# Order of the first key units, halves of a key weight block, a layer norm and a query unit moved, and a bank of its own for the last output columns

## The chip, the cores and the metric

The kernel runs on one core of a Trainium2 chip. The metric is the device time of one execution in microseconds (us). One core has no second die to compare with, so every run here is of one state ("fast" in the records); what remains is a spread of 1 to 2 us between executions of the same kernel. Each number of a kernel is a median of 5 or 6 runs (11 for the kernel before in all calls but the first) unless the text says otherwise. A ratio is the record's own estimate from the fast runs of one call, with its 95% interval; it is not quite the ratio of the medians or of the means quoted.

Names: PE is TensorE's matmul side, PEld its weight load, DVE VectorE, ACT ScalarE, SP the engine that issues most DMAs. In the program a "key unit (i, c)" is eight matmuls that multiply tile i of x (128 rows, normalised and transposed) by block c (512 columns) of the key weights. Value ("V") units are the same with blocks 2 and 3. An "eviction" takes a result out of PSUM, the memory that PE writes, which the program uses in banks of 512 columns; the eviction of a key unit is called "phi" (two instructions on ACT, `e_sb` and `r_sb`, the latter a relu, then two on DVE). psA, psB and psX are tiles in PSUM. The "V run" is the group of products that starts with the first psA near 31 us; xs are sums and differences of blocks of x that DVE makes for it, and a "weight sum" (`w_sums`) is the same for weights.

## The reference, cut to what matters

```python
h  = x + A(layernorm(x))          # linear attention: qkv projection, phi, kv sums, output projection
h2 = h + B(layernorm(h))          # token MLP: w1, gelu, w2
# x: (1, 2048, 1024); wqkv: (1024, 3072); w1: (2048, 3584); w2: (3584, 2048); all bf16
```

The change touches the first 25 us (layer norm of the first four tiles and their key units), two points between 25 and 45 us, and the last product of the second MLP matrix. The rest of the program's instruction order is the same in both kernels.

## The kernel before: the parts that matter

The head. Tiles 0 to 3 are normalised on DVE, transposed on PE, copied out of PSUM, and multiplied. "pin" fixes the program order on every engine.

```python
xs = {0: load_x(0, True)}; xs[1] = load_x(1)
for k0 in (0, hk):                                   # key block 0, in halves of 512 KB
    nc.sync.dma_start(wkv[:, k0:k0 + hk, 0:CW], wqkv_v[:, k0:k0 + hk, D:D + CW])
for i in range(2, 4):
    xs[i] = load_x(i)
for c in range(1, 2 * NDC):                          # key block 1 whole (1 MB), then the V blocks
    nc.sync.dma_start(wkv[:, :, c * CW:(c + 1) * CW], wqkv_v[:, :, D + c * CW:D + (c + 1) * CW])
# ... (tiles 4 and 5 after c == 1; then the query weights)

warm_up(10)
# ... statistics and normalisation of tile 0
transpose_in(0)                  # 8 PE transposes; first copy on ACT, second on DVE
pin(ln[1][1](1)); pin(ln[1][2]()); stats(1)
k_parts(0, 0, lo_k)              # first four matmuls of unit (0,0)
# ... normalise tile 1
transpose_in(1)
phis = [k_parts(0, 0, hi_k)]     # last four
for i in (1, 2):
    # ... statistics of tile i + 1
    phis.append(k_parts(i, 0))
    # ... normalise tile i + 1
    transpose_in(i + 1)
    # ... (i == 2: evictions, and the first weight sum on DVE)
    phis.append(k_parts(i - 1, 1))
# ... proj_unit(3, 0), w_sums, ln_stats(4), proj_unit(2, 1), load_biases
ln_finish(G0)                    # ACT: Ln, Exp of tile 4; DVE: normalise; DMA transpose
proj_unit(3, 1, pin)
# ... two PSUM buffers from here on
proj_unit(0, NDC, pin)           # V unit
```

Later, ahead of the V run:

```python
ln_finish(G0 + 2)
load_next(2 * G0)
q_fill()                         # a query unit and its two ACT evictions
```

The last product, cut into 384 and 128 columns in one PSUM bank:

```python
def m7(self, cuts=(0, CW)):
    for a, b in zip(cuts, cuts[1:]):
        self.mm(7, self.X, False, True, cols=slice(a, b))
        self.evac(0, 0, self.X, a, b)
# ...
pend.m7((0, CW - P, CW))
```

## Time and profile before

| | before |
|---|---|
| time, first three runs | 581.31 us (580.81 to 581.78) |
| span of the profiled execution | 578.7 us |
| PE busy | 569.4 us, 98% |
| PE not busy | 9.3 us |

The head of the page of the kernel before (busy us, share of the span, instructions, by engine):

```profile
span 578.7 us, 7486 instructions
PE 569.4 (98%) x2832; PEld 267.2 (46%) x2854; DVE 385.7 (67%) x752; ACT 211.9 (37%) x432; POOL 1.8 (0%) x8
```

PE is the limit, and a change that removes no matmul can only close its gaps. The list of waits of PE in the kernel before names them (total us, times, longest):

```profile
PE tp L668 <- DVE xn L402: 2.0, 2, 1.0
...
PE psX L228 <- DVE ot_5119 L193: 0.7, 1, 0.7
PE psB L499 <- ACT psB L512: 0.5, 1, 0.5
PE acc_t L423 <- ACT r_sb L161: 0.4, 1, 0.4
```

PE's timeline of the kernel before (start, duration, operation, count, and in brackets the idle time ahead of it with what ended it) places them:

```profile
6.05 0.72 PE L668 MATMUL tp<-ident,xn 128*128 128x128 bf16 x8 [0.98 <-DVE xn L402]
7.13 1.04 PE L423 MATMUL acc_t<-wkv,xnT 128*128 128x512 bf16 x4 [0.35 <-ACT xnT L678]
9.15 0.72 PE L668 MATMUL tp<-ident,xn 128*128 128x128 bf16 x8 [0.98 <-DVE xn L402]
9.71 2.75 PE L423 MATMUL acc_t<-wkv,xnT 128*128 128x512 bf16 x12
...
26.08 5.34 PE L423 MATMUL acc_t<-wkv,xnT 128*128 128x512 bf16 x24 [0.36 <-ACT r_sb L161]
31.26 1.03 PE L499 MATMUL psA<-wkv,xnT 128*128 128x512 bf16 x4
...
45.08 1.02 PE L499 MATMUL psB<-pqT,xs 128*128 128x512 f16 x4 [0.55 <-ACT psB L512]
...
571.61 2.44 PE L228 MATMUL psX<-gO,sa 128*128 128x384 f16 x14
574.76 0.94 PE L228 MATMUL psX<-gO,sa 128*128 128x128 f16 x14 [0.71 <-DVE ot_5119 L193]
```

A 512-column matmul is drawn 0.379 us long, but in a stream the next one starts 0.216 us later: 12 matmuls from 9.71 are drawn as 2.75, that is 11 x 0.216 + 0.379. The Trainium skill gives both lengths ("TensorE: Matmul & The Clock Gate", sections "Single matmul latency" and "Back-to-back issue gap": (398 + 512)/2.4 = 379 ns, and 512/2.4 + 2.5 = 216 ns), and this trace agrees with both. Only the 216 ns is a measurement, though: by its own legend the profile models the ends of matmuls, so the 0.379 us is how long it draws them.

### The profile page before, as it was taken

The page shows a single profiled execution, that of the slowest core. Times are in us where ns is not written, and L with a number is a line of the kernel's source. Part 1 is how long each engine was busy: PE and PEld are TensorE (multiplying, and loading weights), DVE is VectorE, ACT ScalarE, POOL GpSimd, SP SyncE. Part 2 cuts the span into 40 slices and gives each one's busy share as a digit, 9 for nine tenths or more (in the row PEclk, how much of TensorE's full clock was granted, in tenths as well). Part 3 has the DMA queues.
Part 4 walks back from the last instruction along what each step waited for, and adds up shares of the span by engine and source line. Part 5 has one row for each costly group of instructions (what it writes and reads, how often), then busy time and mean ns, then how long its engine had stood idle before and what let it go on. Part 6 is the DMA issues. An engine that isn't in the chain of part 4 may idle for free.

```text
span 578.7 us, 7486 instructions
## 1 busy us (share of the span) xinstructions
PE 569.4 (98%) x2832; PEld 267.2 (46%) x2854; DVE 385.7 (67%) x752; ACT 211.9 (37%) x432; POOL 1.8 (0%) x8
## 2 busy tenths in 40 slices
PE   7999999999999999999999999999999999999997
PEld 3444444455555444444444444444444444444443
DVE  6897887556767889876666666567765456455543
ACT  4647777656668777333222322223000000000000
POOL 1000000000000000000000000000000000000000
PEclk9999999999999999999999999999999999999999
DMA  8943431139438952242224322204966436521101
GB/s 283 361 83 75 91 73 37 20 116 271 69 73 172 283 165 92 73 129 72 74 80 126 85 74 72 74 0 109 226 193 172 130 100 172 149 78 46 36 28 36
DMA packets 109811, 66.55 MB, mean 115 GB/s; under 512 B 31810, under 2 KB 101712, under 8 KB 109776
## 3 DMA queue, kind: packets, MB, share of 16 engines
q1 hardware_dynamic: 109568, 65.94, 42.8%
q8 instruction: 22, 0.36, 0.3%
q10 hardware_dynamic: 144, 0.13, 0.1%
q14 instruction: 13, 0.11, 0.1%
q0 software_dynamic: 64, 0.01, 0.0%
HBM read 50.34 MB, written 8.39 MB: 101 GB/s over the span
## 4 chain that ended last, share of the span: by engine, by line
PE 96%; DVE 2%; ACT 1%; issue 0%; DMA 0%
PE psX L228 17%; PE psW L228 17%; PE psZ L228 17%; PE acc_t L904 9%; PE acc_t L757 9%; PE psY L228 8%; PE psB L499 4%; PE psA L499 4%; PE psC L499 4%; PE acc_t L423 3%; PE psE L499 2%; PE nd_ps L855 1%; DVE st L392 1%; PE kvps_464 L452 1%; PE kvps_465 L452 0%
## 5 line engine op out<-in xcount | busy, mean ns | idle before, releaser
L228 PEld LDWEIGHTS <-sa 128*128 128x128 f16 x1134 | 110.5, 98 | 132.5 <-issue 0.9
L223 DVE TENSOR_TENSOR sa<-w1p 128x1024 f16<-128x1024 bf16 x70 | 47.9, 685 | 20.0 <-PE psX L228 12.4
L757 PE MATMUL acc_t<-xnT,wq_sb 128*128 128x512 bf16 x248 | 57.1, 379 | 0.3
L904 PE MATMUL acc_t<-wo_sb,pqT 128*128 128x512 bf16 x250 | 55.7, 379 | 0.3
L223 DVE TENSOR_TENSOR sa<-w2p 128x1792 f16<-128x1792 bf16 x40 | 43.4, 1084 | 10.1 <-PE psW L228 7.6
L904 PEld LDWEIGHTS <-pqT 128*128 128x128 bf16 x256 | 24.8, 98 | 29.1
L757 PEld LDWEIGHTS <-wq_sb 128*128 128x128 bf16 x256 | 24.5, 98 | 27.4
L164 DVE TENSOR_SCALAR e_sb<-e_sb 128x512 bf16<-128x512 bf16 x64 | 18.5, 290 | 26.9 <-ACT e_sb L160 26.4
L264 DVE TENSOR_TENSOR tt<-psW,dd 128x512 f32<-128x512 f32 x22 | 15.2, 692 | 29.2 <-PE psW L228 29.2
L228 PEld LDWEIGHTS <-w1p 128*128 128x128 bf16 x224 | 21.9, 98 | 26.4
L228 PEld LDWEIGHTS <-w2p 128*128 128x128 bf16 x224 | 21.9, 98 | 26.4
L259 DVE TENSOR_TENSOR psY<-psX,dd 128x512 f32<-128x512 f32 x22 | 15.4, 699 | 27.5 <-PE psX L228 27.5
L160 ACT ACTIVATE e_sb<-acc_t 128x512 bf16<-128x512 f32 x40 | 23.9, 597 | 24.2 <-PE acc_t L757 20.7
L499 PEld LDWEIGHTS <-xs 128*128 128x128 f16 x208 | 20.0, 98 | 23.6 <-DVE xs L485 0.8
L269 DVE TENSOR_TENSOR tt<-tt,psZ 128x512 f32<-128x512 f32 x22 | 15.1, 688 | 18.0 <-PE psZ L228 17.9
L228 PE MATMUL psZ<-hT_2226,w1p 128*128 128x512 f16 x112 | 26.8, 379 | 0.0
L499 PE MATMUL psA<-wkv,xnT 128*128 128x512 bf16 x98 | 26.4, 379 | 0.3
L228 PE MATMUL psW<-hE,sa 128*128 128x512 f16 x112 | 26.6, 379 | 0.0
L228 PE MATMUL psX<-hT_2225,sa 128*128 128x512 f16 x112 | 26.6, 379 | 0.0
L228 PE MATMUL psW<-hT_2227,w1p 128*128 128x512 f16 x112 | 26.5, 379 | 0.0
L228 PE MATMUL psZ<-hO,sa 128*128 128x512 f16 x112 | 26.5, 379 | 0.0
L228 PE MATMUL psX<-hO,sa 128*128 128x512 f16 x112 | 26.5, 379 | 0.0
(256 smaller groups left out, 838.9 us busy)
## 6 DMA issues: line engine op xcount, KB each, us to landing
w1p<-in_B_w_dram SPq DMA_DIRECT2D x14, 1024.0 KB, 5.6
w2p<-in_B_w_dram SPq DMA_DIRECT2D x8, 1792.0 KB, 8.1
xr<-in_A_x_dram SPq DMA_DIRECT2D x16, 256.0 KB, 3.4
x_sb<-in_A_x_dram SPq DMA_DIRECT2D x15, 256.0 KB, 4.1
wkv<-in_A_wqkv_dram SPq DMA_DIRECT2D x3, 1024.0 KB, 9.7
wq_sb<-in_A_wqkv_dram SPq DMA_DIRECT2D x2, 1024.0 KB, 12.6
wo_sb<-in_A_wo_dram SPq DMA_DIRECT2D x2, 1024.0 KB, 6.5
wkv<-in_A_wqkv_dram SPq DMA_DIRECT2D x2, 512.0 KB, 5.7
```

Of the source, the lines that this page charges most:

```text
L160: pin(nc.scalar.activation(e_sb[:], src, ACT.Exp))
L164: pin(nc.vector.tensor_scalar(e_sb[:], e_sb[:], 1.0, PHI_EPS, ALU.min, ALU.add))
L223: return nc.vector.tensor_tensor(t, a, b, op)
L228: nc.tensor.matmul(ps[:, cols], lhsT=sa[:, k, :], rhs=mv(k)[:, cols], start=(start and k == 0), stop=(stop and k == self.nk - 1), skip_gro ...
L259: nc.vector.tensor_tensor(self.Y[:], self.X[:], self.d[:], ALU.add)
L264: nc.vector.tensor_tensor(self.t[:], self.W[:], self.d[:], ALU.add)
L269: nc.vector.tensor_tensor(self.t[:], self.t[:], self.Z[:], ALU.subtract)
L392: return nc.vector.bn_stats(st[:, c, :], x_sb[:, c * CW:(c + 1) * CW])
L423: mm = nc.tensor.matmul(pp[:, 0:CW], lhsT=xnT[:, kt, i * P:(i + 1) * P], rhs=wkv[:, kt, c * CW:(c + 1) * CW], start=(kt == 0), stop=(kt == ...
L499: pin(nc.tensor.matmul(ps[:], lhsT=lhs[:, k, :], rhs=rhs[:, k, :], start=(start and k == 0), stop=(k == hk2 - 1), skip_group_check=True,))
L757: nc.tensor.matmul(qp[:, 0:SW], lhsT=wq_sb[:, kt, j * P:(j + 1) * P], rhs=xnT[:, kt, u * SW:(u + 1) * SW], start=(kt == 0), stop=(kt == ND ...
L904: nc.tensor.matmul(ap_[:, 0:CW], lhsT=pqT[:, j, i * P:(i + 1) * P], rhs=wo_sb[:, j, dc * CW:(dc + 1) * CW], start=(j == 0 and not SEED_RES ...
```

## The change

The intent: give PE work while it waits for the second tile's normalisation (all of unit (0,0), and an order in which key units lie between the groups of transposes); make unit (0,1) possible earlier by loading key block 1 in two halves ahead of tile 3; take two waits of PE for ACT away by moving a layer norm and a query unit; and let the last 128 columns run without waiting for the eviction of the 384 ahead of them.

```diff
-        def m7(self, cuts=(0, CW)):
-            for a, b in zip(cuts, cuts[1:]):
-                self.mm(7, self.X, False, True, cols=slice(a, b))
-                self.evac(0, 0, self.X, a, b)
+        def m7(self):
+            for a, b, ps in self.parts:      # parts: (0, 384, X), (384, 512, tile of its own)
+                self.mm(7, ps, False, True, cols=slice(a, b))
+                self.evac(0, 0, ps, a, b)
 ...  (m5 adds into each part; only the last product is cut)
+            xs[2] = load_x(2)
+            for k0 in (0, hk):
+                nc.sync.dma_start(wkv[:, k0:k0 + hk, CW:D], wqkv_v[:, k0:k0 + hk, D + CW:2 * D])
+            for i in range(3, G0 + 2):
+                xs[i] = load_x(i)
 ...  (V blocks and query weights follow)
-                    pin((nc.vector.tensor_copy if i == 0 and h == 1 else nc.scalar.copy)(*t))
+                    pin(nc.scalar.copy(*t))
 ...
-            k_parts(0, 0, lo_k)
+            k_unit(0, 0)
             ...  normalise tile 1
             transpose_in(1)
+            ln_stats(2); stats(2)
+            k_unit(1, 0)
+            norm_halves(2); phi_act((0, 0))
+            k_unit(0, 1)
+            phi_act((1, 0))
+            transpose_in(2)
+            ln_stats(3); stats(3)
+            phi_dve((0, 0)); w_sums(kmov, slice(0, 1)); norm_halves(3)
+            phi_dve((1, 0)); phi_act((0, 1))
+            k_unit(1, 1)
+            transpose_in(3)
 ...  (then units (2,0), (3,0), (2,1), (3,1))
             load_biases(trp)
-            ln_finish(G0)
             proj_unit(3, 1, pin)
 ...
             proj_unit(0, NDC, pin)
+            ln_finish(G0)
 ...
+            q_fill()
             ln_finish(G0 + 2)
             load_next(2 * G0)
-            q_fill()
```

More of the change, by code (lines that the diff above doesn't have):

```diff
@@ L265, in m4, with m5 @@
             self.evac(1, 0, self.W)
-        def m5(self):
+        def m5(self, cut=None):
             self.mm(5, self.Z, False, True)
             nc.vector.tensor_tensor(self.t[:], self.t[:], self.Z[:], ALU.subtract)
-            nc.vector.tensor_tensor(self.X[:], self.X[:], self.t[:], ALU.add)
+            self.parts = [(0, CW, self.X)]
+            if cut is not None:
+                self.parts = [(0, cut, self.X), (cut, CW, psw.tile([P, BANK], F32, tag="w", name="psX2"))]
+            for a, b, ps in self.parts:
+                nc.vector.tensor_tensor(ps[:, a:b], self.X[:, a:b], self.t[:, a:b], ALU.add)
             self.evac(0, 1, self.Z)
@@ L275, in m6 @@
             self.evac(1, 1, self.Y)
-        def m7(self, cuts=(0, CW)):
-            for a, b in zip(cuts, cuts[1:]):
-                self.mm(7, self.X, False, True, cols=slice(a, b))
-                self.evac(0, 0, self.X, a, b)
+        def m7(self):
+            for a, b, ps in self.parts:
+                self.mm(7, ps, False, True, cols=slice(a, b))
+                self.evac(0, 0, ps, a, b)
     def moving(E, O, T1, T3, T4):
@@ L292, in moving, with run_pair @@
         }
-    def run_pair(st, nxt, split, pending):
+    def run_pair(st, nxt, split, pending, cut=None):
         if split:
@@ L311, in run_pair @@
             nxt.asum(2)
-        st.m5()
+        st.m5(cut)
         if nxt is not None:
@@ L649 @@
             )
-            for i in range(2, 4):
+            xs[2] = load_x(2)
+            for k0 in (0, hk):
+                nc.sync.dma_start(wkv[:, k0:k0 + hk, CW:D], wqkv_v[:, k0:k0 + hk, D + CW:2 * D])
+            for i in range(3, G0 + 2):
                 xs[i] = load_x(i)
-            for c in range(1, 2 * NDC):
+            for c in range(2, 2 * NDC):
                 nc.sync.dma_start(wkv[:, :, c * CW:(c + 1) * CW], wqkv_v[:, :, D + c * CW:D + (c + 1) * CW])
-                if c == 1:
-                    for i in range(G0, G0 + 2):
-                        xs[i] = load_x(i)
             for c in range(NDC):
@@ L661 @@
             halves = (slice(0, CW), slice(CW, D))
-            ln[0] = ln_chunks(0, xs.pop(0))
             def transpose_half(i, h):
@@ L688, with norm_halves, phi_act, phi_dve @@
             pps = {}
-            pin(ln[0][1](0))
-            pin(ln[0][1](1))
-            pin(ln[0][2]())
+            def norm_halves(i):
+                for h in range(2):
+                    pin(ln[i][4](halves[h]))
+            def phi_act(*keys):
+                for key in keys:
+                    phis[key][0]()
+            def phi_dve(*keys):
+                for key in keys:
+                    phis[key][1]()
+            def k_unit(i, c):
+                phis[i, c] = k_parts(i, c)
+            phis = {}
+            ln_stats(0)
             stats(0)
@@ L694 @@
             pin(ln[1][1](0))
-            for h in range(2):
-                pin(ln[0][4](halves[h]))
+            norm_halves(0)
             transpose_in(0)
@@ L700 @@
             stats(1)
-            k_parts(0, 0, lo_k)
-            for h in range(2):
-                pin(ln[1][4](halves[h]))
+            k_unit(0, 0)
+            norm_halves(1)
             transpose_in(1)
-            phis = [k_parts(0, 0, hi_k)]
-            for i in (1, 2):
-                ln[i + 1] = ln_chunks(i + 1, xs.pop(i + 1))
-                pin(ln[i + 1][1](0))
-                pin(ln[i + 1][1](1))
-                pin(ln[i + 1][2]())
-                stats(i + 1)
-                phis.append(k_parts(i, 0))
-                for h in range(2):
-                    pin(ln[i + 1][4](halves[h]))
-                phis[2 * i - 2][0]()
-                if i == 2:
-                    phis[1][0]()
-                transpose_in(i + 1)
-                if i == 2:
-                    phis[0][1]()
-                    phis[1][1]()
-                    w_sums(kmov, slice(0, 1))
-                phis.append(k_parts(i - 1, 1))
-            phis[2][1]()
-            for act, dve in phis[3:]:
-                act()
-                dve()
-            proj_unit(3, 0, pin)
-            w_sums(kmov, slice(1, 2))
+            ln_stats(2)
+            stats(2)
+            k_unit(1, 0)
+            norm_halves(2)
+            phi_act((0, 0))
+            k_unit(0, 1)
+            phi_act((1, 0))
+            transpose_in(2)
+            ln_stats(3)
+            stats(3)
+            phi_dve((0, 0))
+            w_sums(kmov, slice(0, 1))
+            norm_halves(3)
+            phi_dve((1, 0))
+            phi_act((0, 1))
+            k_unit(1, 1)
+            transpose_in(3)
+            phi_dve((0, 1))
+            k_unit(2, 0)
+            phi_act((1, 1))
+            phi_dve((1, 1))
+            k_unit(3, 0)
+            phi_act((2, 0))
+            phi_dve((2, 0))
+            w_sums(kmov, slice(1, 2))
+            k_unit(2, 1)
+            phi_act((3, 0))
+            phi_dve((3, 0))
+            phi_act((2, 1))
+            phi_dve((2, 1))
             ln_stats(G0)
-            proj_unit(2, 1, pin)
             load_biases(trp)
-            ln_finish(G0)
             proj_unit(3, 1, pin)
@@ L1015 @@
         cur.evac.prefetch()
-        run_pair(cur, nxt, False, pend)
+        run_pair(cur, nxt, False, pend, None if nxt is not None else CW - P)
         pend = cur
         cur = nxt
-    pend.m7((0, CW - P, CW))
+    pend.m7()
 _INS = ['A_x', 'A_wqkv', 'A_wo', 'B_x', 'B_w1', 'B_b1', 'B_w2', 'B_b2']
```

## The prediction

> **What bounds it now.** TensorE. The page gives PE 569.4 us busy of a 578.7 us span (98%) at full granted clock; the chain that ended last is 96% PE. The change removes no matmul, so only PE's 9.3 us of gaps can shrink. The list of waits and PE's timeline show those in reach: 1.0 us before the second tile's transposes (at 9.15, waiting for its normalisation) and about 0.4 us hidden in the groups around it; 0.36 us at 26.08 (a V unit waits for ScalarE's relu); 0.55 us at 45.08 (psB waits for ScalarE's copy); 0.71 us in the last product (128 columns wait for the eviction of 384). Together 3.0 us, 0.5%.
>
> **What the change does, costed.**
> 1. Tail. The last 128 columns get their own bank; their 14 matmuls (0.94 us) no longer wait for the 0.62 us eviction: gain 0.6 to 0.7. The Trainium skill, "PSUM — Partial Sum Buffer", section "PSUM bank collisions raise a hardware error", says two engines may not touch one bank at once even at disjoint columns; the trace shows that wait, 0.71 us at 574.76.
> 2. Head. Unit (0,0) now lies wholly before the second transposes and fills the 1.0 us hole; tile 0's second copy moves from DVE to ACT, freeing DVE 0.8 us earlier. New gaps: (a) unit (0,0)'s second half needs the second half of the first weight block, landing about 8.4 (DMA view): about 0.4 us. (b) Unit (1,0) follows its own transposes at once and exposes a copy: 0.35 to 0.45. (c) Tile 3's load now queues behind 1 MB of weights. That block took 3.0 us (x 3 landed 9.7, the block 12.7), so x 3 lands about 12.7. Then, in DVE order, statistics 1.3, aggregate 0.2, a phi pair 0.7, a weight sum 1.2, half a normalisation 0.4: tile 3's transposes at about 16.6, while PE is free at about 15.8; 0.5 to 1.0 us lost. The skill, "DMA: Bandwidth & Descriptors", section "Queues, rings and completion order", says an engine takes a row's descriptors in order; the landings agree. Half loads let unit (0,1) start at 11.9 (half lands about 10.6). Net of the head: between 0.5 lost and 1.0 gained, most likely 0.
> 3. LayerNorm of tile 4 finishes one V unit later: removes the 0.36 us.
> 4. The query unit ahead of tile 6's LayerNorm lets ScalarE do two evictions inside its 2.9 us wait for statistics: psB's copy comes earlier, gains 0.45.
>
> **Total.** 0.65 + 0 + 0.36 + 0.45, about 1.4 us: **580.0 us**, range **578.8 to 581.0**. Faster by over 2% (11.6 us) would exceed all of PE's idle time: 0.01. Within 2%: 0.98. Slower by over 2%: 0.01.
>
> **What would show it.** PE's timeline: no wait inside the last product; no idle at the first V units and at psB near 44; unit (0,0) as eight matmuls with a short DMA wait in the middle; a copy wait before unit (1,0); idle before tile 3's transposes, put down to DVE's normalisation. DVE's timeline: tile 3's first statistics at about 12.7, released by DMA. PE busy the same within 1 us.
>
> **What would make it wrong.** x 3 landing before the block ahead of it (1 us more gained, 579); the second weight half arriving after unit (0,1) reaches it (1 us lost, 581); ScalarE's new order only moving its waits to the next PSUM reuse; the last output's DMA, not the matmuls, setting the end.

## The result, and the profile after

In the first call: 579.30 us (579.17 to 580.38, 6 runs) against 581.00 us (580.59 to 581.78, 6 runs); ratio 0.9973, 95% interval 0.9960 to 0.9986. The changed kernel was run in two more calls, with ratios 0.9985 (0.9974 to 0.9997) and 0.9985 (0.9968 to 1.0002). Over its 17 runs the median is 579.89 us. So the gain is real but small, somewhere between 0.8 and 1.7 us, 1.3 us if the means of all runs are taken (579.96 against 581.26, the latter over 39 runs of the kernel before). The prediction was 580.0. Part of the spread is PE's clock: the record lists the granted clock of each run but those of the kernel before in the first call, and runs at 0.994 to 0.997 are slower than the others of their kernel (the kernel before: 582.0 us over 10 such runs, 581.0 over 23 at 0.999 or 1.000). At 0.999 or 1.000 the changed kernel takes 579.60 us (13 runs), which is 1.4 us less. This figure does not show everything: it reads 1.000 for the profile of tail_mid (below), whose first four matmuls of unit (0,0) took 1.89 us, against 1.04 us in tail_mid_again.

The profile after fell in the slowest of its six runs (580.38 us), in which the first weights landed late. Compare it with the profile before by stretches, not by absolute times. Head of the page and PE's list of waits, kernel after:

```profile
span 578.6 us, 7489 instructions
...
PE acc_t L427 <- DMA wkv<-in_A_wqkv_dram: 1.6, 2, 1.2
...
PE tp L670 <- DVE xn L406: 0.9, 2, 0.5
PE acc_t L427 <- ACT xnT L680: 0.5, 1, 0.5
PE psB L503 <- DVE xs L489: 0.3, 1, 0.3
```

The waits for ACT's relu, for psB's copy and for the eviction of the last product are gone. In their place stand waits for weights, for a copy, and for xs. PE's timeline of the kernel after:

```profile
8.27 1.02 PE L427 MATMUL acc_t<-wkv,xnT 128*128 128x512 bf16 x4 [1.25 <-DMA wkv<-in_A_wqkv_dram]
9.67 1.02 PE L427 MATMUL acc_t<-wkv,xnT 128*128 128x512 bf16 x4 [0.37 <-DMA wkv<-in_A_wqkv_dram]
10.53 0.61 PE L670 MATMUL tp<-ident,xn 128*128 128x128 bf16 x8
11.59 3.41 PE L427 MATMUL acc_t<-wkv,xnT 128*128 128x512 bf16 x15 [0.45 <-ACT xnT L680]
...
17.75 0.72 PE L670 MATMUL tp<-ident,xn 128*128 128x128 bf16 x8 [0.35 <-DVE xn L406]
...
32.36 1.03 PE L503 MATMUL psA<-wkv,xnT 128*128 128x512 bf16 x4
...
36.34 1.04 PE L503 MATMUL psB<-wo_sb,xs 128*128 128x512 f16 x4 [0.28 <-DVE xs L489]
...
572.46 2.44 PE L228 MATMUL psX<-gO,sa 128*128 128x384 f16 x14
574.73 0.94 PE L228 MATMUL psX_5224<-gO,sa 128*128 128x128 f16 x14
```

The first line is bad luck of this run: in the profile before, the same half of block 0 had landed 1.5 us sooner (5.0 us after its issue instead of 6.5) and unit (0,0) began at 7.13. The next lines are the new order. The hole of 1.0 us before the second transposes is filled. But unit (0,0) now waits in its middle for the second half of block 0; unit (1,0) waits for the copy of its own transposes; and tile 3's transposes wait for DVE. DVE's timeline of the kernel after shows why tile 3's transposes wait:

```profile
14.02 1.29 DVE L396 BATCH_NORM_STATS2 st<-x_sb 128x6 f32<-128x512 bf16 x2 [0.79 <-DMA x_sb<-in_A_x_dram]
...
16.15 1.22 DVE L477 TENSOR_TENSOR pqT<-wkv 128x2048 f16<-128x2048 bf16 x1
17.28 0.73 DVE L406 TENSOR_SCALAR xn<-x_sb,mv,rstd 128x512 bf16<-128x512 bf16 x2
```

Tile 3's load arrives behind the weights, and its normalisation stands behind a weight sum of 1.22 us. At the tail, from the first part's start to the second's it is now 574.73 - 572.46 = 2.27 us, against 3.15: 0.88 us gained.

### The profile page after: what moved, and what is told of

The parts are those of the page before. It is cut to its first block, busy times and chain, and to the rows that moved or that the text cites. A ratio compares the mean times of both kernels' runs of the same rounds, so it can differ in the third digit from the quotient of the medians.

```text
span 578.6 us, 7489 instructions
## 1 busy us (share of the span) xinstructions
PE 570.0 (99%) x2832; PEld 267.5 (46%) x2854; DVE 385.6 (67%) x752; ACT 212.6 (37%) x433; POOL 1.8 (0%) x8
## 4 chain that ended last, share of the span: by engine, by line
PE 93%; DMA 3%; DVE 2%; SPq 1%; issue 1%; ACT 0%; DVEq 0%
PE psZ L228 17%; PE psW L228 17%; PE psX L228 17%; PE acc_t L922 9%; PE acc_t L775 9%; PE psY L228 8%; PE psB L503 4%; PE psC L503 4%; PE psA L503 4%; PE psE L503 2%; DMA x_sb<-in_A_x_dram 2%; PE nd_ps L873 1%; DMA xr<-in_A_x_dram 1%; DVE wo_sb L477 1%; DVE st L396 0%
```

## The experiments

All outputs are right. To take out the landing of the weights I measure the head from the first matmul of unit (0,0) to the V run's first psA matmul ("head stretch"): 31.26 - 7.13 = 24.13 us before, 32.36 - 8.27 = 24.09 us after.

### First call: the change taken apart

**after_again**: the changed kernel, unedited.

> The changed kernel once more, for a second profile: the first one fell in its slowest run (580.4 us against 579.2 to 579.9), in which the first weight halves landed over 1 us later than in the profile of before. Theory (the three parts add up: tail 0.9, ScalarE reordering 0.6, head about 0): 1.3 to 1.8 us below the kernel before. If the weights land early again, unit (0,0) starts at about 7.2 instead of 8.3, and the V run's first psA at about 31.0 instead of 32.4.

Measured: 580.19 us against 581.16; ratio 0.9985 (0.9974 to 0.9997). The profile again had late weights (unit (0,0) began at 8.01), and the head stretch was 24.03 us. The expected 1.3 to 1.8 us was not reached: 1.0 by the medians. Three of its five runs had the clock at 0.997, against 2 of 11 of the kernel before, which may be a part of it.

**tail_only**: the kernel before with the bank alone.

```diff
-    pend.m7((0, CW - P, CW))
+    pend.m7()                    # with parts in two tiles, as in the change
```

> Before plus the separate bank alone. Theory: the second part of the last product starts 2.27 us after the first instead of 3.15, so the time falls by 0.85 to 0.9 us. Rival (the last output's DMA sets the end, or the extra add delays the product): 0 to 0.3 us.

Measured: 580.69 us; ratio 0.9983 (0.9971 to 0.9995), 0.9 us by the means. In its trace the two parts run as one group of 28 matmuls with nothing between. From psA (32.65) to the start of the last eviction (576.26) it took 543.61 us against 575.74 - 31.26 = 544.48 us before: 0.87 us gained. The span ends 2.92 us after the start of that eviction, against 2.94 before, so the end of the program moved with it. The theory holds; the rival (the last DMA sets the end) falls.

**mid_only**: the kernel before with the two ACT moves alone.

```diff
-            ln_finish(G0)
             proj_unit(3, 1, pin)
...
             proj_unit(0, NDC, pin)
+            ln_finish(G0)
...
+            q_fill()
             ln_finish(G0 + 2)
             load_next(2 * G0)
-            q_fill()
```

> Before plus the two moves alone: LayerNorm of tile 4 one V unit later, a query unit ahead of LayerNorm of tile 6. Theory: both waits of TensorE for ScalarE (0.36 and 0.55 us) vanish, 0.6 to 0.9 us less. Rival (they come back as other waits, as the 0.28 us for xs in the profile after suggests): 0.3 us or less.

Measured: 580.30 us; ratio 0.9982 (0.9970 to 0.9994), 1.0 us by the means. Its weights landed early as in the profile before, so the two can be laid side by side. Head stretch 30.67 - 7.10 = 23.57 us against 24.13, 0.56 us less. Of this 0.04 us is lost ahead of the place where the move can act (from unit (0,0) to the small transposes of the biases it is 21.89 - 7.10 = 14.79 us against 21.96 - 7.13 = 14.83), so the layer norm's move is worth 0.52 us. From psA to the last eviction 574.90 - 30.67 = 544.23 us against 544.48: the query unit's move is worth only 0.25 us. Both old waits are gone, but the list of waits of this kernel has a new one:

```profile
PE psB L499 <- DVE xs L485: 0.3, 1, 0.3
```

PE now comes to psB before DVE has the sums of tiles 2 and 3. So the rival was half right: 0.28 us of the 0.55 came back. That wait belongs to these moves and not to the new head, since this kernel has the old head.

**head_only**: the kernel before with the new order of units and loads alone, the layer norm of tile 4 left in its old place.

```diff
+            # new order of units and loads as in the change
             load_biases(trp)
+            ln_finish(G0)
             proj_unit(3, 1, pin)
```

> Before plus the new order of the first units and of their loads alone. Theory (the filled hole of 1.0 us is given back as waits for the second weight half, for the copies, and for tile 3's normalisation): between 0.3 us faster and 0.5 us slower. Rival (the head is the main gain): 0.8 us or more faster.

Measured: 582.67 us; ratio 1.0021 (1.0008 to 1.0034): 1.5 us slower by the means, worse than either theory had it. About half of that is the clock: three of its six runs had it at 0.996 or 0.997, and the other three took 581.58 to 582.08 us, against 580.77 to 581.37 for the kernel before at 0.999 or 1.000 in the same call, 0.7 us slower by the means. The list of waits, from one of the runs at 0.997, says why it is slower at all:

```profile
PE acc_t L423 <- ACT r_sb L161: 1.5, 1, 1.5
PE acc_t L423 <- DMA wkv<-in_A_wqkv_dram: 1.5, 1, 1.5
```

The second line is the late landing of the first weights again. The first is the wait that was 0.36 us in the kernel before, now 1.54; how large it is at full clock no trace shows. In the new order tile 4's statistics come later on DVE; ACT stands at tile 4's logarithm for 2.56 us, as its timeline shows, and the eviction that PE needs is behind it:

```profile
28.08 0.29 ACT L398 ACTIVATE lnv<-mv,eps_ln 128x1 f32<-128x1 f32 x1 [2.56 <-DVE mv L395]
```

The layer norm's move is therefore not an independent 0.5 us but part of the new head: without it the new order loses. (PE's clock fell to half for a while in this profile; see the end.)

### Second call: what the head gives back

**tail_mid**: the kernel before with the bank and the two ACT moves; old head and old loads.

> Before plus the separate bank plus the two ScalarE moves, with the old order of the first units and loads. Theory (the new head brings nothing of its own): 1.5 to 2.0 us below the kernel before, as fast as the changed kernel or faster. Rival (the head is part of the gain once LayerNorm of tile 4 is out of its way): no more than 1.0 us below the kernel before.

Measured: 579.60 us; ratio 0.9971 (0.9957 to 0.9986), 1.7 us by the means. That is as much as the changed kernel ever showed. The theory holds, the rival falls: the new head is not part of the gain.

**split_first**: the changed kernel, unit (0,0) cut again.

```diff
-            k_unit(0, 0)
+            k_parts(0, 0, lo_k)
             norm_halves(1)
             transpose_in(1)
+            phis[0, 0] = k_parts(0, 0, hi_k)
```

> The changed kernel with unit (0,0) cut again at the second tile's transposes: four matmuls before, four after. Theory (the wait for the second weight half and the bare copy before unit (1,0) are what the head gives back): the waits of 0.3 us for weights and 0.45 us for the copy vanish, the V run's first psA comes about 0.7 us earlier for the same landing of the first weight half, and the time is 0.3 to 0.8 us below the changed kernel's. Rival (the copy is not what unit (1,0) waits for, or the normalisation of tile 1 comes too late): no change.

Measured: 579.54 us; ratio 0.9968 (0.9954 to 0.9982). Inside the spread of the changed kernel, although both waits did vanish: the timeline shows 19 matmuls from 9.03 as one group. (One wait of 0.25 us from start to start is hidden in it, ahead of the fifth matmul of unit (0,1), at 12.73; the second half of block 1 landed then, 9.0 us after its issue at 3.7.) The saved time came back at tile 3, whose wait grew from 0.35 to 1.21 us:

```profile
9.03 4.51 PE L427 MATMUL acc_t<-wkv,xnT 128*128 128x512 bf16 x19
13.59 0.61 PE L670 MATMUL tp<-ident,xn 128*128 128x128 bf16 x8
14.04 1.89 PE L427 MATMUL acc_t<-wkv,xnT 128*128 128x512 bf16 x8
17.14 0.72 PE L670 MATMUL tp<-ident,xn 128*128 128x128 bf16 x8 [1.21 <-DVE xn L406]
```

Head stretch 31.75 - 7.69 = 24.06 us, as before the edit. My theory was wrong in one thing: the two waits were real, but were not what set the head's length. Tile 3's normalisation was.

**late_wsum**: the changed kernel, the weight sum after the normalisation.

```diff
             phi_dve((0, 0))
-            w_sums(kmov, slice(0, 1))
             norm_halves(3)
+            w_sums(kmov, slice(0, 1))
```

> The changed kernel with the first weight sum (1.22 us of DVE) after tile 3's normalisation instead of before it. Theory: the 0.36 us wait before tile 3's transposes and the 0.1 us inside them vanish, 0.3 to 0.5 us less than the changed kernel. Rival (tile 3's load is what is late): no change.

Measured: 579.49 us; ratio 0.9966 (0.9953 to 0.9979). No wait before tile 3's transposes is left in the list, but the bracket misleads here. PE's timeline of late_wsum:

```profile
14.26 1.89 PE L427 MATMUL acc_t<-wkv,xnT 128*128 128x512 bf16 x8
16.24 0.72 PE L670 MATMUL tp<-ident,xn 128*128 128x128 bf16 x8
```

Eight matmuls take 1.73 us from start to start, so PE was free at 15.99 and still waited 0.25 us. DVE's normalisation of tile 3 no longer stands behind the weight sum, but now it waits 0.85 us for ACT's rstd. From tile 3's first statistics (12.71) to its transposes it is 3.53 us, against 3.73 in the profile after: the move is worth 0.2 us, less than expected. Head stretch 30.85 - 7.55 = 23.30 us against 24.0; the other 0.5 us is luck of the landings: the second half of block 0 was there in time, and unit (0,0) did not wait in its middle. By the total time alone this kernel can't be told from the changed one.

**whole_block**: the changed kernel with key block 1 as one load of 1 MB.

```diff
-            for k0 in (0, hk):
-                nc.sync.dma_start(wkv[:, k0:k0 + hk, CW:D], wqkv_v[:, k0:k0 + hk, D + CW:2 * D])
+            nc.sync.dma_start(wkv[:, :, CW:D], wqkv_v[:, :, D + CW:2 * D])
```

> The changed kernel with the second key weight block loaded whole, at the same place. Theory: unit (0,1) waits for all of it, about 12.1 to 13.3 us after the start, while TensorE is there at 13.3 to 13.5 by the profile after: no wait, or under 0.3 us, so the halves are worth nearly nothing: within 0.3 us of the changed kernel. Rival: 0.5 us or more slower.

Measured: 580.12 us; ratio 0.9979 (0.9966 to 0.9993). Unit (0,1) does not wait, and the head stretch is 31.57 - 7.51 = 24.06 us, the same as the changed kernel's 24.03 to 24.09. The halves of the second block bring nothing that these traces show.

What these traces have in common explains all three results. In after, after_again, after_third (below), split_first and whole_block tile 3's first statistics start between 12.51 and 14.02 us, released by the landing of its load. In every one of the five the transposes of tile 3 start 3.73 or 3.74 us later, and psA another 14.61 or 14.62 us after them. So with the new head psA comes 18.35 us after tile 3 has landed, whatever unit (0,0) waited for before.

### Third call: old head against new on one chip, and a better one

**after_third** is the changed kernel and **tail_mid_again** is tail_mid, both unedited.

> The changed kernel beside the three others of this call, on one chip. Theory (old head and new head are equal in total): 1.2 to 1.8 us below the kernel before, within 0.4 us of tail_mid_again. Rival (the new head gains): 0.5 us or more below tail_mid_again.

> Tail and the two ScalarE moves with the old head, on the same chip as after_third. Theory: 1.3 to 1.9 us below the kernel before. From the first matmul of unit (0,0) to the V run's first psA 23.6 us as in tail_mid, against 24.0 to 24.1 in after_third.

Measured: 579.70 us (ratio 0.9985, 0.9968 to 1.0002) and 579.77 us (ratio 0.9977, 0.9965 to 0.9989). No difference that the runs show. This time the first weights landed early in both profiles. PE's timeline of after_third:

```profile
6.95 1.04 PE L427 MATMUL acc_t<-wkv,xnT 128*128 128x512 bf16 x4 [0.41 <-ACT xnT L680]
8.17 1.02 PE L427 MATMUL acc_t<-wkv,xnT 128*128 128x512 bf16 x4 [0.18 <-DMA wkv<-in_A_wqkv_dram]
9.03 0.61 PE L670 MATMUL tp<-ident,xn 128*128 128x128 bf16 x8
10.10 3.41 PE L427 MATMUL acc_t<-wkv,xnT 128*128 128x512 bf16 x15 [0.46 <-ACT xnT L680]
...
16.24 0.72 PE L670 MATMUL tp<-ident,xn 128*128 128x128 bf16 x8 [0.35 <-DVE xn L406]
...
30.86 1.03 PE L503 MATMUL psA<-wkv,xnT 128*128 128x512 bf16 x4
```

and of tail_mid_again:

```profile
7.28 1.04 PE L427 MATMUL acc_t<-wkv,xnT 128*128 128x512 bf16 x4 [0.35 <-ACT xnT L682]
9.30 0.72 PE L672 MATMUL tp<-ident,xn 128*128 128x128 bf16 x8 [0.98 <-DVE xn L406]
9.86 2.75 PE L427 MATMUL acc_t<-wkv,xnT 128*128 128x512 bf16 x12
...
30.85 1.03 PE L503 MATMUL psA<-wkv,xnT 128*128 128x512 bf16 x4
```

Head stretch 23.91 us with the new head, 23.57 us with the old: the new head costs 0.34 us in this pair (0.2 to 0.5 us over the other traces of the two heads with the layer norm moved, 23.91 to 24.09 and 23.57 to 23.68). psA itself comes at the same time in both, because unit (0,0) happened to start 0.33 us earlier in after_third. Start to start, with 0.216 us for a matmul and 0.445 us for eight transposes of this size (9.30 to 9.86 shows 0.56 with a short wait in it; 12.45 to 12.89 in the same trace shows 0.44), the old head loses 1.16 us at the second transposes and 0.11 in them. The new one loses 0.36 us in the middle of unit (0,0), 0.62 before unit (1,0), 0.50 before tile 3's transposes (unit (1,1) began at 14.01) and 0.11 in them: 1.59 against 1.27 us.

**reorder**: three moves in the changed kernel's head.

```diff
-            k_unit(0, 0)
+            k_parts(0, 0, lo_k)
             ...
             transpose_in(1)
+            phis[0, 0] = k_parts(0, 0, hi_k)
             ...
             phi_dve((0, 0))
-            w_sums(kmov, slice(0, 1))
             norm_halves(3)
+            w_sums(kmov, slice(0, 1))
             ...
             k_unit(1, 1)
-            transpose_in(3)
             k_unit(2, 0)
+            transpose_in(3)
+            k_unit(2, 1)
             k_unit(3, 0)
             ...  (evictions follow their units)
```

> The changed kernel with three moves in the head: unit (0,0) cut at the second transposes, the first weight sum after tile 3's normalisation, and tile 3's transposes one unit later with unit (2,1) behind them. Theory (these are the waits that ate the filled hole): no wait between unit (0,0) and the V units but the copy waits at its start; 22.7 to 23.1 us from unit (0,0)'s first matmul to psA, 0.8 to 1.2 us less than the changed kernel. Rival (the first weight landing alone sets the time of the head): no change.

**reorder_xs**: the same, and the sums of tiles 2 and 3 earlier on DVE.

```diff
+            x_sums(1)
             w_sums(vmov, slice(2, 4))
             proj_unit(1, NDC + 1, pin)
             ln_finish(G0 + 1)
-            x_sums(1)
```

> The same, with the V run's sums of tiles 2 and 3 ahead of the second pair of V weight sums on DVE. Theory: the wait of 0.3 us for xs before psB, and the late start hidden in front of it, vanish too: 0.3 to 0.4 us below reorder, 2.5 us or more below the kernel before. Rival: the weight sums now come late for psE or psC and the wait moves there.

Measured: reorder 578.85 us, ratio 0.9961 (0.9949 to 0.9974); reorder_xs 578.97 us, ratio 0.9961 (0.9947 to 0.9975), fastest run 577.75 us. Both are 2.3 to 2.4 us below the kernel before by the means, and about 0.8 us below the changed kernel of the same call by the medians. At a clock of 0.999 or 1.000 they take 578.57 us (4 runs) and 578.23 us (3 runs), against 579.54 us (5 runs) for after_third. The waits are gone from the traces: this is the whole list of PE's waits of reorder_xs but for one line, the start of the warm-up matmuls.

```profile
PE tp L670 <- DVE xn L406: 1.3, 1, 1.3
...
PE acc_t L427 <- ACT xnT L680: 0.4, 1, 0.4
PE acc_t L427 <- issue: 0.2, 1, 0.2
```

The first two are those of tile 0, at the very start, which no order of later units can touch. The last is most likely a missing record: the group behind it shows 39 matmuls of 40, and the gap is of the size of one.

The expected 22.7 to 23.1 us from unit (0,0) to psA was not seen in these two profiles (31.92 - 8.10 = 23.82 and 31.24 - 7.25 = 23.99 us), for a reason that has nothing to do with the order: PE's clock. The table of stretches of reorder_xs (us, length and PE busy with matmuls, granted clock, DMA share, GB/s):

```profile
6.80:7.40 0.60, 0.24 (x3) 1.00 1.00 364
7.40:10.60 3.20, 3.20 (x15) 0.50 1.09 370
```

For 3.2 us PE ran at half the clock, which costs 1.6 us; 23.99 - 1.6 = 22.4 us would have been the stretch at full clock, an estimate that supposes that no wait would have come back. The mean granted clock of a run shows it: 1 - 1.6/577 is 0.997, and of the 11 runs of these two kernels the four at 0.997 took 578.8 to 579.9 us, the seven at 0.999 or 1.000 from 577.75 to 579.2 us. Both profiles fell in runs at 0.997, and a PE that is 1.6 us late finds its inputs ready more easily; so the traces alone do not show that every wait is gone at full clock. The times at full clock do show the gain. How much of it each of the three moves brings was not separated. Between reorder and reorder_xs the times show no difference; that the wait for xs vanished is seen in the trace alone.

## Why the prediction was right

The total and its range held: 580.0 us predicted, 579.30 us in the first call and 579.89 us over 17 runs, range 578.8 to 581.0. Point by point:

| term | predicted gain | measured in the traces | from |
|---|---|---|---|
| bank for the last columns | 0.65 | 0.87 | before, tail_only |
| layer norm of tile 4 later | 0.36 | 0.52 | before, mid_only |
| query unit before tile 6's layer norm | 0.45 | 0.25 | before, mid_only |
| head: order and loads | 0 (0.5 lost to 1.0 gained) | 0.34 lost | after_third, tail_mid_again |
| sum | 1.46 | 1.30 | |

That the sum came so close is partly luck. The terms were off by 0.22 and 0.16 us one way and by 0.20 and 0.34 us the other, and these errors nearly cancel. The mechanisms were right, as the points below show; the sizes less so.

1. *PE bounds it, only gaps can shrink.* Right. The traces' sum of 1.30 us agrees with the 1.3 us between the means of all runs and the 1.4 us at full clock.
2. *Tail.* The mechanism was right, the size too small. The term was read from the bracket, 0.71 us, and cut down a little; the true delay from start to start was 0.88 us, because the drawn length of the matmul ahead overlaps the next. The Trainium skill's rule on banks (in the prediction) is followed by the program: with separate banks the wait is gone in every trace that has them. That a collision would do harm no run here shows, as no kernel had one.
3. *Layer norm of tile 4.* Same mis-sizing: 0.36 in the bracket and 0.163 hidden make 0.52; measured 0.52. What I had not seen is that this move is a condition for the new head: without it head_only waits 1.54 us there.
4. *Query unit.* ACT's wait was removed as said, and with the hidden part the old gap was 0.55 + 0.16 = 0.71 us. But the prediction's own last warning came true in another form: the wait moved to DVE's xs, 0.28 us in the bracket and 0.44 with the hidden part. 0.71 - 0.44 = 0.27 us, as measured (0.25).
5. *Head.* The three new waits were all there, by name and place. In after_third: second half of block 0 0.36 us (said 0.4), the bare copy before unit (1,0) 0.46 in the bracket (said 0.35 to 0.45), tile 3 0.50 us start to start (said 0.5 to 1.0). Tile 3's statistics started at 12.51, released by its load (said 12.7, worked out from the landings before). The Trainium skill's order of descriptors ("DMA: Bandwidth & Descriptors", section "Queues, rings and completion order") agrees: moved behind 1 MB of weights, x 3 came about 3 us later than its 9.7 in the profile before. The best guess of a head worth nothing was 0.34 us too kind, inside the range that was given for it.
6. *Not foreseen.* How much the landing of the first weights varies between executions, and the half clock.

That tile 3 and not the two earlier waits set the head's length is shown by split_first, which lost those two and gained nothing in the head stretch, and by the five traces in which psA follows tile 3's landing by 18.35 us. Left open: what would happen with a longer warm-up, which might keep the clock up in the head, was not run.

## What to carry to other kernels

Size a gap on TensorE from start to start of the matmuls, not from the idle time in front of a bar: here the three brackets from which the terms were read were each short by the same 0.16 us, and in late_wsum a wait of 0.25 us had no bracket at all. When a hole is filled by moving work forward, look at what the work then waits for, and take away the last of the waits first: split_first removed two of three and gained nothing, reorder removed all three and ran another 0.8 us faster. On an engine whose program order is fixed, as ACT's is here, a small instruction that waits holds up all evictions behind it (2.56 us at the logarithm of a layer norm in head_only), so place it behind evictions that are due, not ahead of them.

## What the Trainium skill lacked or had wrong

- "TensorE: Matmul & The Clock Gate", section "Back-to-back issue gap", gives a sustained spacing of about 131 ns for 512 columns in a real stream of weight loads and matmuls, beside 216 ns for the isolated gap. In this case's streams it is 216 ns: in tail_mid_again the 40 matmuls from 22.20 to 30.85 (39 of them recorded) took 8.65 us.
- The same page's table in Part 1 ties the loss of the clock to an idle window of about 3.4 us. In reorder_xs the clock halved at 7.4 us though PE's longest idle time until then was 1.3 us; in after, with an idle time of 1.25 us ahead of unit (0,0), it stayed up. So a whole idle window was not needed here, and what decided stays open. The table is not all that the page has: Part 1 also describes a kernel that loses the clock through short idle times between groups of matmuls. That the half clock then lasts about 3.4 us agrees (3.2 us in full at half clock, back by 11.0), and so does the page's warning that it varies between runs: 0.997 against 1.000 between executions of one kernel, about 1.6 us.
- No page that I read says that the idle time ahead of a matmul in the profile is short by drawn length less pitch, 0.163 us at 512 columns, though the first page above has both numbers.
- "DMA: Bandwidth & Descriptors" has nothing on a slump at the start of an execution. The same queue of loads moved 330 GB/s or more from 3.6 to 4.8 us in mid_only and 109 to 236 GB/s in after. The first weight half landed 5.0 us after its issue in one and 6.5 us in the other. These slices of 0.3 us of the DMA view, mid_only first, then after, show it (slices 13 to 16). The profile before slumped too, to 160 to 184 GB/s from 5.1 to 6.3 us, and its half landed after 5.0 us, so a slump alone does not make it late; the cause stays open.

```profile
GB/s 0 0 0 0 0 20 61 58 362 389 420 396 330 362 333 352 365 375 376 329 299 365 379 393 379 376 376 372 358 365 372 362 355 352 345 355 358 393 328 382
```

```profile
GB/s 0 0 0 0 0 10 119 96 294 389 341 376 154 126 109 236 324 362 348 355 319 363 376 386 404 382 379 382 352 362 362 335 358 348 348 358 372 355 389 376
```
